# One block of expert 0 moved between the scores and y's products, in the sixth to tenth round of the attention stage

## The chip, the cores and the metric

The kernel runs on one core of one Trainium2 chip. The metric is the device time of one execution in microseconds (us); several executions are timed and their median is given. A profile of one further execution lists every instruction with its start and its duration. The engines are named as in the profile: PE is the matrix engine, PEld its weight loads, DVE the vector engine, ACT the scalar engine, POOL the general engine, SP the engine that issues most transfers.

## The reference

A linear attention with a decaying state gives `x`, and a mixture of eight experts with a balanced gate is applied to `x`.

```python
for t in range(S):                       # B, H, S, D = 4, 8, 768, 48
    cur = np.einsum('bhd,bhe->bhde', u[None] * kt, vt)
    y[:, :, t] = np.einsum('bhd,bhde->bhe', rt, state + cur)
    state = w[None, :, :, None] * state + np.einsum('bhd,bhe->bhde', kt, vt)
...
logits = x @ w_gate                      # x: 3072 x 384, 8 experts, F = 1024
P = np.exp(logits - logits.max())
for _ in range(8):
    P /= P.sum(1, keepdims=True) + 1e-09
    P /= P.sum(0, keepdims=True) + 1e-09
    P *= N / E
...
for e in range(E):
    h = np.maximum(x @ w1[e], 0.0)
    out += P[:, e:e + 1] * (h @ w2[e])
```

## The kernel before

The program has two stages. The first computes the attention; the second computes experts 1 to 7, with the products of PE back to back. Expert 0 is worked on during the first stage already, in small blocks that are strewn between the attention's steps. Every engine works through its own instructions strictly in the order in which the program wrote them (all calls go through a wrapper that keeps the program's order), and engines wait for each other at semaphores.

**Rounds.** The attention runs over 24 tiles of 128 tokens (6 per batch entry) in a loop over `i`. "Round 5" below is the round with `i == 5`, the sixth. Round `i` works on several tiles at once. On PE its order is: the transposes of tile `i+1` (`prT`, `pkT`, in `stage_b`), the scores of tile `i` (`pA`, in `stage_c`), the products of `y` for tile `i-1` (`py` from the state `S`, in `state_part`, where the tile isn't the first of its batch entry; then `py` from `vn` and the masked scores `at`, in `scores_part`), the state's new products of tile `i` (`py` from `vn` and `kp`, in `state_product`, where it isn't the last of its batch entry), and then blocks of expert 0.

**Expert 0's blocks.** A block is one entry of the list `units`, and `work(n)` issues the next n of them. A first-product block (`g1_unit`) is nine matmuls of 128x384 into a bank `ph`; a second-product block (`g2_half`) is twelve of them into a bank `po`. The bank `ph` comes from a pool with two buffers, so each `ph` block writes the bank of the last but one before it. A `ph` bank is read twice: ACT writes the high half `hb` from it, then DVE writes the low half (`hb<-ph,hb`). With `hold=True` these two reads are not issued at once but kept; in the next round `leave(0)` issues the ACT ones ahead of the copies `rT`, `kT`, and `leave(1)` the DVE ones after the row `dg` and ahead of the masked copy `at`. If a `po` block needs an `hb` that is still kept, `settle` issues what is kept on the spot.

**DVE in a round.** DVE's order is: `xsc` (low half of tile `i-2`), `dg`, the kept `hb` rows, the two masked copies `at<-mask,pA`, in some rounds a split of expert 0's weights (`ws`), then `x<-py,rk` (two rows), the state `S`, the maximum `xm`, three short rows that end with `xs`, and `kp` of a later tile. `x` is y's sum for tile `i-1` and needs the round's `py`. In some rounds `ws` comes behind `xs`.

**Which block is where.** Round 4 issues one block at its end, rounds 5 to 9 issue two, round 10 issues three; from round 11 on one stands between scores and y's products and two at the end. Blocks are numbered by group and chunk: `ph_0_3` is chunk 3 of group 0. Rounds 5 to 9 take `ph_0_1` and `ph_0_2`; `ph_0_3` and `po_0_0`; `po_1_0` and `po_2_0`; `ph_1_0` and `ph_1_1`; `ph_1_2` and `ph_1_3`.

Of the kernel before, what the change touches and what calls it, by code (L numbers as in the profile page):

```python
# [33 lines left out]
def rwkv_sinkhorn_moe(  # L34
# [37 lines left out]
    NE = 4  # L72
# [204 lines left out]
    def leave(n):  # L277
        for f in exits[n]:
            f()
        exits[n].clear()  # L280
        if n:
            owed.clear()
# [6 lines left out]
    def whole(gen):  # L289
        for _ in gen:  # L290
            pass
# [33 lines left out]
    def load_part(tt, nm, src):  # L325
        b, c = divmod(tt, NCHB)
        if tt == 3 and nm != "v":
            t_ = part(hb3, F32, 2880 + "rk".index(nm) * H * D, (H, D))
        else:
            t_ = ld.tile([P, H, D], F32, tag=nm + "n", name=f"{nm}n_{tt}", bufs=5 if nm == "v" else 3)  # L330
        Q.dma_start(t_, src[b, :, c * C : (c + 1) * C, :].rearrange("h t d -> t h d"))
        loads.setdefault(tt, {})[nm] = t_
# [197 lines left out]
    def prep(tt):  # L530
        ld_ = loads[tt]
        st[tt] = {}
        G.tensor_tensor(rp_[tt % 2][:, :, :D], ld_["r"], rt4, op=ALU.mult)
        if 0 < tt - 2 < NE:
            bonus(tt - 2)
        (G if 2 <= tt <= 2 * NE else V).tensor_tensor(kp_[tt % 3][:, :, :D], ld_["k"], kt4, op=ALU.mult)
        if tt == 2:
            bonus(0)

    def bonus_dot(tt):  # L540
        ld_ = loads[tt]
        rk = rk0
        if tt:
            rk = at2.tile([P, H, D], F32, tag="rk", name=f"rk_{tt}", bufs=3)
            G.tensor_tensor(rk, ld_["r"], ld_["k"], op=ALU.mult)
        G.tensor_tensor(rk, rk, ub, op=ALU.mult)
        st[tt]["rk"] = rk

    def bonus(tt):
        vn = loads[tt]["v"]  # L550
        dg = at2.tile([P, H], F32, tag="dg", name=f"dg_{tt}")
        V.tensor_reduce(dg, st[tt]["rk"], axis=AX.X, op=ALU.add)
        av = st[tt].pop("rk")
        G.tensor_tensor(av, vn, dg.unsqueeze(2).broadcast_to([P, H, D]), op=ALU.mult)
        if tt >= NE:
            aq = av.rearrange("p h d -> p (h d)")
            G.tensor_tensor(aq, aq, xadd(tt), op=ALU.add)
        st[tt]["av"] = av

    def stage_b(tt):  # L560
        d = st[tt]
        for nm, src in (("rT", rp_[tt % 2]), ("kT", kp_[tt % 3])):
            pool, tag = (ps2, "po") if tt <= NE + 1 else (ps3, "pa")
            pt = pool.tile([P, NPAIR, P], F32, tag=tag, name=f"p{nm}_{tt}")
            sv = src.rearrange("p (a j) d -> p a (j d)", j=2)
            for p_ in range(NPAIR):
                T.transpose(pt[:, p_, :], sv[:, p_, :], ident)
            dst = at2.tile([P, NPAIR, P], F32, tag=nm, name=f"{nm}_{tt}", bufs=3 if nm == "rT" else 2)
            S_.copy(dst, pt)
            d[nm] = dst  # L570

    def stage_c(tt):
        d = st[tt]
        rT, kT = d["rT"], d["kT"]
        at = at_[tt % 2].rearrange("p (a g) c -> p g a c", g=2)
        pas = []
        for g in range(2):
            pa = ps3.tile([P, NPAIR, C], F32, tag="pa", name=f"pA_{tt}_{g}")
            pas.append(pa)
        for a in range(NPAIR):  # L580
            for g in range(2):
                rows = slice(g * HP, g * HP + HP)
                for hs in (slice(0, HP), slice(HP, C)):
                    T.matmul(pas[g][hs, a, :], kT[rows, a, hs], rT[rows, a, :], start=True, stop=True)
        for g in range(2):
            V.copy_predicated(
                at[:, g], maski.unsqueeze(1).broadcast_to([P, NPAIR, C]), pas[g]
            )
# [38 lines left out]
    def addends(tt):  # L627
        d = st[tt]
        d["py"] = y_banks(tt)
        for n, x_ in enumerate((xadd(tt).rearrange("p (h d) -> p h d", d=D), d["av"])):  # L630
            xg = x_.rearrange("p (a g) d -> p g a d", g=2)
            for g in range(2):
                T.matmul(d["py"][g], ident, xg[:, g], start=(n == 0), stop=False, skip_group_check=True)
        if tt + 1 < NE:
            T.matmul(d["pu"], ident, st[tt + 1]["S"], start=False, stop=False, skip_group_check=True)

    def state_part(tt):
        d = st[tt]
        if tt % NCHB == 0:
            return  # L640
        fresh = "py" not in d
        if fresh:
            d["py"] = y_banks(tt)
        for p_ in range(NPAIR):
            for g in range(2):
                rows = slice(g * HP, (g + 1) * HP)
                for hs in (slice(0, HP), slice(HP, C)):
                    T.matmul(
                        d["py"][g][hs, p_, :], d["rT"][rows, p_, hs], d["S"][rows, p_, :],
                        start=(fresh and p_ == 0), stop=False, skip_group_check=True,  # L650
                    )
# [176 lines left out]
    def work(n, hold=False):  # L828
        held[0] = hold
        for _ in range(n):  # L830
            if units:
                whole(units.pop(0))
        held[0] = False
# [7 lines left out]
    def n_steps(i):  # L841
        return (0, 0) if i < 10 else (2, 2) if i < 21 else (3, 2)
# [6 lines left out]
    def run(i, place):  # L849
        for f in hooks.pop((i, place), []):  # L850
            f()
# [45 lines left out]
    def send_x(i):  # L897
        if 2 <= i <= NTT + 1 and i != TH + 1:
            scale_x(i - 2)
            if i > TH:  # L900
                stage_e(i - 2)
            emitted[0] = i - 1

    for i in range(NTT + 3):
        if 1 <= i <= NE:
            stage_b(i + 1)
        run(i, "turned")
        if i + 2 < NTT and i != TH + 1:
            prep(i + 2)
        if i > NE:  # L910
            send_x(i)
        leave(0)
        if i + 1 < NTT:
            bonus_dot(i + 1)
        if NE < i < NTT - 1:
            stage_b(i + 1)
        if 1 <= i <= NE:
            addends(i - 1)
        if i <= NE:
            send_x(i)  # L920
        n = i + 5 if i < 2 else i + 4
        if i != 2 and n < NTT:
            load_part(n, "r", r)
            load_part(n, "k", k)
        if i == 0:
            load_part(3, "v", v)
        if i == 8:
            Q.dma_start(wg, w_gate.rearrange("(c p) e -> p c e", p=P))
        run(i, "loads")
        if NE <= i < NTT:  # L930
            bonus(i)
        leave(1)
        run(i, "early")
        if i < NTT:
            stage_c(i)
        if i > 10:
            work(1)
        run(i, "masked")
        if 1 <= i <= NTT:
            state_part(i - 1)  # L940
            scores_part(i - 1)
        if 2 <= i <= TH + 1:
            turn_x(i - 2)
        if i < NTT:
            state_product(i)
        if 1 <= i <= NTT:
            sum_x(i - 1)
        if i < NTT:
            state_sum(i)
        if 1 <= i <= NTT:  # L950
            bound_x(i - 1)
        if i > NTT:
            work(2)
        run(i, "middle")
        if 2 <= i < NTT - 2:
            load_part(i + 2, "v", v)
        for _ in range(n_steps(i)[0]):
            prepare()
        if i <= NTT:
            if i > TH:  # L960
                work(1 if i == 4 else 3 if i == 10 else 2, hold=i < 10)
            elif i == 0:
                S_.copy(onesb, ones)
                S_.copy(ident16, ident)
        run(i, "end")
        for _ in range(n_steps(i)[1]):
            prepare()
        if i == TH:
            prep(i + 3)
            scale_x(TH - 1)  # L970
            run(i, "last")
            units += [g1_unit(0, fc, 0) for fc in range(FHC)]
            units += [g2_half(0, t, 0, 0) for t in range(TH)]
        done = i - 2
        if TH <= done < NTT and done % TH == TH - 1:
            po_ = done // TH
            for p_, j in ((1, 0), (0, 1), (1, 1)) if po_ == 1 else ((po_, 0), (po_, 1)):
                turn[0] += 1
                g1 = [g1_unit(p_, fc, turn[0]) for fc in range(j * FHC, (j + 1) * FHC)]
                units += merged(g1, [g2_half(*a_) for a_ in pend])  # L980
                pend = [(p_, t, j, turn[0]) for t in range(TH)]
# [402 lines left out]
    for s in range(NS):  # L1384
        tasks = stage_tasks(s)
        for g in range(NG):
            for j in range(2):
                for n, nxt in enumerate(g1_slots(s, g, j)):
# [3 lines left out]
                    i = j * NPR + n  # L1392
# [37 lines left out]
```

## Time and profile before

| | |
|---|---|
| median of 3 runs | 1513.77 us (1513.34 to 1514.48) |
| the profiled execution: its time | 1514.62 us |
| the profiled execution: its span | 1513.1 us |
| DVE busy over the span | 1010.1 us (67%) |
| ACT busy over the span | 674.8 us (45%) |
| POOL busy over the span | 586.8 us (39%) |

The profiled execution's own time is 1.5 us longer than its span, and 0.85 us above the median. Rows of a timeline begin with start and duration in us, then engine, operation, tile written and tiles read, shapes, and count of merged instructions; in brackets stands the idle time ahead of them and who ended it. "issue" is idle time for which the profile names no one. A row's duration of merged matmuls includes the drain of the last one, so the step from one row's start to the next row's start is what a part costs on PE.

### The profile page before, as it was taken

How to read it: one execution, taken by the hardware profiler on the slowest of the kernel's cores; microseconds unless marked ns; L12 is line 12 of the kernel's file. 1: busy time of each engine (PE TensorE's matmuls, PEld its weight loads, DVE VectorE, ACT ScalarE, POOL GpSimd, SP SyncE). 2: the span in 40 equal slices, each digit the busy share in tenths (PEclk: the TensorE clock that was granted, in tenths of full speed). 3: DMA queues.
4: the chain of work that ended last, by engine and by line, in shares of the span. 5: the costliest groups of instructions: out<-in, count | busy, mean ns of one | idle time of the engine just before them, and what ended most of it. 6: DMA issues, size and time to landing. Idle time of an engine off the chain costs nothing.

```text
span 1513.1 us, 28843 instructions
## 1 busy us (share of the span) xinstructions
PE 1501.1 (99%) x11654; PEld 846.7 (56%) x11656; DVE 1010.1 (67%) x1678; ACT 674.8 (45%) x1206; POOL 586.8 (39%) x687
## 2 busy tenths in 40 slices
PE   9999999999999999999999999999999999999999
PEld 7767766555555555555555555555555555555555
DVE  7998859676666666666676666666565666566464
ACT  6534425345354544445454544445353544444320
POOL 8878966200224243342425243242424233242200
PEclk9999999999999999999999999999999999999999
DMA  8965532212255576657666666655554454555434
GB/s 164 163 115 119 113 89 78 79 46 75 81 106 62 83 130 93 123 80 128 90 88 114 91 127 92 116 61 99 61 94 56 60 99 59 97 61 96 58 95 130
DMA packets 184840, 142.69 MB, mean 94 GB/s; under 512 B 107137, under 2 KB 178562, under 8 KB 184706
## 3 DMA queue, kind: packets, MB, share of 16 engines
q0 software_dynamic: 44928, 61.36, 32.6%
q1 hardware_dynamic: 139568, 79.48, 20.3%
q8 instruction: 91, 1.49, 0.4%
q14 instruction: 43, 0.35, 0.1%
q10 hardware_dynamic: 210, 0.00, 0.0%
HBM read 55.39 MB, written 80.23 MB: 90 GB/s over the span
## 4 chain that ended last, share of the span: by engine, by line
PE 95%; DVE 3%; POOL 1%; ACT 1%; issue 1%; ACTq 0%; POOLq 0%; DVEq 0%
PE po L30 49%; PE bZ L30 12%; PE bY L30 12%; PE ph L30 5%; PE bA L30 5%; PE bB L30 5%; PE py L30 2%; PE bC L30 2%; PE pA L30 1%; PE prT L30 1%; PE pkT L30 1%; POOL rk L30 0%; DVE hb L30 0%; DVE wms L30 0%; ACT hbx L30 0%
## 5 line engine op out<-in xcount | busy, mean ns | idle before, releaser
L30 PE MATMUL po<-ws,hbx 128*128 128x384 f16 x3360 | 736.8, 326 | 0.0
L30 POOL DMA_DIRECT2D accd<-stg x288 | 250.5, 870 | 694.8 <-ACT stg L30 673.9
L30 PEld LDWEIGHTS <-hbx 128*128 128x128 f16 x3360 | 328.8, 98 | 291.1
L30 PEld LDWEIGHTS <-ws 128*128 128x128 f16 x3096 | 301.0, 98 | 247.4 <-issue 3.5
L30 ACT ACTIVATE hbx<-tb 128x512 f16<-128x512 f32 x224 | 141.0, 630 | 450.8 <-DVE tb L30 450.8
L30 PE MATMUL po<-ws,hb 128*128 128x384 f16 x1248 | 323.2, 326 | 0.5 <-DVE hb L30 0.5
L30 DVE TENSOR_TENSOR tb<-bY,tb 128x512 f32<-128x512 f32 x168 | 116.2, 692 | 176.6 <-PE bY L30 175.0
L30 ACT ACTIVATE stg<-po,pe 128x384 f32<-128x384 f32 x312 | 179.1, 574 | 122.7 <-PE po L30 95.0
L30 PE MATMUL bZ<-xv,ws 128*128 128x512 f16 x840 | 227.0, 379 | 0.7 <-DVE tb L30 0.7
L30 PE MATMUL bY<-xv,ws 128*128 128x512 f16 x840 | 227.0, 379 | 0.0
L30 DVE TENSOR_TENSOR tb<-bZ,tb 128x512 f32<-128x512 f32 x168 | 115.5, 687 | 135.4 <-PE bZ L30 135.4
L30 PEld LDWEIGHTS <-hb 128*128 128x128 f16 x1248 | 121.1, 98 | 95.2 <-DVE hb L30 1.3
L30 POOL TENSOR_TENSOR ucb<-rawb 128x256 f32<-128x256 f32 x84 | 77.5, 972 | 112.7 <-DMA rawb<-in_moe_w_dram 112.7
L30 DVE TENSOR_TENSOR tb<-bB,tb 128x512 f32<-128x512 f32 x112 | 77.5, 692 | 49.2 <-PE bB L30 47.3
L30 PE MATMUL ph<-hbx,ws 128*128 128x384 f16 x576 | 104.2, 326 | 0.6 <-issue 0.3
L30 DVE SCALAR_TENSOR_TENSOR hb<-tb,hbx 128x512 f16<-128x512 f32 x112 | 77.3, 690 | 24.6 <-ACT hbx L30 19.5
L30 PE MATMUL bB<-xv,ws 128*128 128x512 f16 x336 | 90.8, 379 | 0.0
L30 PE MATMUL bA<-xv,ws 128*128 128x512 f16 x336 | 90.8, 379 | 0.0
L30 DVE SCALAR_TENSOR_TENSOR hbx<-tb,hbx 128x512 f16<-128x512 f32 x112 | 78.1, 698 | 14.7 <-ACT hbx L30 10.4
L30 ACT COPY tb<-bZ 128x512 f32<-128x512 f32 x56 | 32.8, 586 | 65.5 <-PE bZ L30 65.4
L30 ACT ACTIVATE hb<-ph 128x384 f16<-128x384 f32 x64 | 31.0, 489 | 58.6 <-PE ph L30 58.2
L30 DVE SCALAR_TENSOR_TENSOR hb<-ph,hb 128x384 f16<-128x384 f32 x64 | 34.8, 550 | 29.2 <-ACT hb L30 28.7
(181 smaller groups left out, 1492.9 us busy)
## 6 DMA issues: line engine op xcount, KB each, us to landing
accd<-stg POOLq DMA_DIRECT2D x288, 192.0 KB, 3.7
rawb<-in_moe_w_dram SPq DMA_DIRECT2D x28, 768.0 KB, 7.9
e0d<-stg SPq DMA_DIRECT2D x48, 192.0 KB, 1.9
hb<-e0d SPq DMA_DIRECT2D x48, 192.0 KB, 3.7
vn<-in_v_dram SPq DMA_DIRECT2D x24, 192.0 KB, 4.4
accd<-stg SPq DMA_DIRECT2D x24, 192.0 KB, 1.8
accd<-hb POOLq DMA_DIRECT2D x24, 192.0 KB, 4.7
rawb<-accd SPq DMA_DIRECT2D x24, 192.0 KB, 2.4
```

What stands on the lines that cost most here:

```text
L30: return lambda *a, **k: self.tc.keep_in_program_order(f(*a, **k))
```

## The change

In rounds 5 to 9 the first of the two blocks is issued ahead of y's products, still with its reads kept for later; only one is left at the round's end. Rounds 0 to 4 and from 10 on are as they were.

```diff
@@ -933,8 +933,8 @@
         run(i, "early")
         if i < NTT:
             stage_c(i)
-        if i > 10:
-            work(1)
+        if i > NE and i != 10:
+            work(1, hold=i < 10)
         run(i, "masked")
         if 1 <= i <= NTT:
             state_part(i - 1)
@@ -958,7 +958,7 @@
             prepare()
         if i <= NTT:
             if i > TH:
-                work(1 if i == 4 else 3 if i == 10 else 2, hold=i < 10)
+                work(1 if i < 10 else 3 if i == 10 else 2, hold=i < 10)
             elif i == 0:
                 S_.copy(onesb, ones)
                 S_.copy(ident16, ident)
```

Round 6 on PE, before: `pA` are the scores of tile 6, `py_5` the products of y for tile 5, `ph_0_3` and `po_0_0` the round's blocks.

```order
L30 MATMUL pA_6_1_1149<-rT_6_988,kT_6_995 64x128 x2
L30 MATMUL py_5_0_1168<-S1_179,rT_5_819 64x48 [waits Activation_49]
...
L30 MATMUL py_5_0_1168<-vn_6_961,kp0_173 32x48 x15
L30 LDWEIGHTS ws1_75
L30 MATMUL ph_0_3_1246<-hbx_72,ws1_75 128x384 [waits DVE_49]
...
L30 MATMUL po_0_0_1258<-ws1_75,hb3_73 128x384
```

The same place on PE in the changed program:

```order
L30 MATMUL pA_6_1_1149<-rT_6_988,kT_6_995 64x128 x2
L30 LDWEIGHTS ws1_75
L30 MATMUL ph_0_3_1168<-hbx_72,ws1_75 128x384 [waits DVE_49]
...
L30 MATMUL py_5_0_1178<-S1_179,rT_5_819 64x48 [waits Activation_49]
...
L30 MATMUL py_5_0_1178<-vn_6_961,kp0_173 32x48 x15
...
L30 MATMUL po_0_0_1258<-ws1_75,hb3_73 128x384
```

The nine matmuls of `ph_0_3`, which wait for DVE, have moved from behind y's products to ahead of them; `po_0_0` has stayed.

Round 9 on PE in the changed program, with y's products of tile 8 and the blocks `ph_1_2` and `ph_1_3`:

```order
L30 MATMUL pA_9_1_1618<-rT_9_1435,kT_9_1442 64x128 x2
L30 LDWEIGHTS ws1_75
L30 MATMUL ph_1_2_1637<-hbx_72,ws1_75 128x384 [waits DVE_49]
...
L30 MATMUL py_8_0_1648<-S1_179,rT_8_1288 64x48 [waits Activation_49]
...
L30 MATMUL py_8_0_1648<-vn_9_1400,kp0_173 32x48 x15
L30 LDWEIGHTS ws1_75
L30 MATMUL ph_1_3_1727<-hbx_72,ws1_75 128x384 [waits DVE_49]
```

Here too the first block now stands, with its wait for DVE, ahead of y's products.

Round 9 on DVE in the changed program, from the low half of tile 7 to the sum of tile 8:

```order
L30 SCALAR_TENSOR_TENSOR xsc_7_1582<-x_7_1553,xs_7_1560,xsc_7_1582 128x384 [waits DMAHW1_49,Activation_49]
L30 TENSOR_REDUCE dg_9_1609<-rk_9_1427 128x8 [waits Pool_49]
L30 SCALAR_TENSOR_TENSOR hb3_73<-ph_1_0_1477,hb3_73 128x384 [waits Activation_49]
L30 SCALAR_TENSOR_TENSOR hb3_73<-ph_1_1_1570,hb3_73 128x384 [waits Activation_49]
L30 COPY_PREDICATED at1_177<-mask_168,pA_9_0_1617 128x4x128 [waits PE_49]
L30 COPY_PREDICATED at1_177<-mask_168,pA_9_1_1618 128x4x128 [waits PE_49]
L30 SCALAR_TENSOR_TENSOR ws1_75<-ws0_74,sw0_1_114,ws1_75 128x768 [waits DMAHW6_49,Activation_49]
L30 TENSOR_TENSOR x_8_1714<-py_8_0_1648,rk_8_1280 128x4x48 [waits PE_49,Pool_49]
```

On DVE, ACT, POOL and SP no instruction has moved in any round: only the numbers in names differ from before. The reads of `ph_1_0` and `ph_1_1` stand where they stood.

## The prediction

> **What bounds the kernel now.** First I read the page's head, then a table of stretches around the changed rounds, then the timelines of PE and DVE in them. Rounds are numbered by `i`: round 5 is the sixth.
>
> ```profile
> span 1513.1 us, 28843 instructions
> PE 1501.1 (99%) x11654; PEld 846.7 (56%) x11656; DVE 1010.1 (67%) x1678; ACT 674.8 (45%) x1206; POOL 586.8 (39%) x687
> ...
> 40.00:88.00 48.00, 45.39 (x1084) 33.29 (x1084) 44.97 (x97) 21.45 (x37) 37.84 (x39) 1.00 0.87 157
> 88.00:1513.00 1425.00, 1418.99 (x9758) 785.55 (x9755) 934.65 (x1521) 626.35 (x1115) 514.20 (x603) 1.00 0.52 90
> ...
> 45.00:53.00 8.00, 6.71 (x186) 5.03 (x185) 7.90 (x12) 3.89 (x6) 7.84 (x7) 1.00 1.19 207
> ```
>
> The columns of the stretches are length, then PE, PEld, DVE, ACT and POOL busy. After 88 us PE is busy 1418.99 of 1425 us, so whatever start round 11 gets (87.85 us before) moves the end by as much. Between 40 and 88 us, which holds the five changed rounds and round 10, DVE is as full (44.97 of 48) as PE (45.39). DVE's share of 67% over the span says nothing there: this is the stretch in which both lie on the path by turns.
>
> PE in rounds 5 to 7:
>
> ```profile
> 41.22 1.10 PE L30 MATMUL pA<-rT,kT 64*64 64x128 f32 x32
> ...
> 49.16 0.63 PE L30 MATMUL py<-S,rT 64*64 64x48 f32 x32
> ...
> 51.46 0.33 PE L30 MATMUL py<-vn,at 128*32 128x48 f32 x11 [0.96 <-issue]
> ...
> 52.10 1.64 PE L30 MATMUL ph<-hbx,ws 128*128 128x384 f16 x9
> 53.58 2.25 PE L30 MATMUL po<-ws,hb 128*128 128x384 f16 x12
> 55.66 0.60 PE L30 MATMUL prT<-ident,rp 128*128 128x128 f32 x4
> ```
>
> DVE in the same stretch:
>
> ```profile
> 44.17 0.62 DVE L30 TENSOR_TENSOR x<-py,rk 128x192 f32<-128x192 f32 x2
> ...
> 45.87 3.35 DVE L30 SCALAR_TENSOR_TENSOR ws<-ws,sw,ws 128x768 f16<-128x768 f32 x2
> 49.14 1.37 DVE L30 SCALAR_TENSOR_TENSOR xsc<-x,xs,xsc 128x384 f16<-128x384 f32 x1
> ...
> 50.90 1.01 DVE L30 SCALAR_TENSOR_TENSOR hb<-ph,hb 128x384 f16<-128x384 f32 x2
> ...
> 53.06 0.62 DVE L30 TENSOR_TENSOR x<-py,rk 128x192 f32<-128x192 f32 x2
> ...
> 54.90 0.54 DVE L30 SCALAR_TENSOR_TENSOR hb<-ph,hb 128x384 f16<-128x384 f32 x1
> 55.35 1.30 DVE L30 TENSOR_TENSOR kp<-kn,ktab 128x384 f32<-128x384 f32 x1
> ```
>
> The reader is to see two things. DVE has no bracket in any of these rows: it runs from x of round 5 to the end without a pause. And PE's `ph` of round 6 (52.10) starts 0.7 us after the first `hb<-ph,hb` of the pair is done (50.90 and half of 1.01, 51.40). That DVE row frees the bank which `ph_0_3` writes. Before, the block came late enough not to notice.
>
> PE in rounds 8 to 10, then DVE:
>
> ```profile
> 62.74 0.60 PE L30 MATMUL prT<-ident,rp 128*128 128x128 f32 x4
> ...
> 64.35 1.10 PE L30 MATMUL pA<-rT,kT 64*64 64x128 f32 x32
> ...
> 67.22 0.38 PE L30 MATMUL py<-vn,kp 128*32 128x48 f32 x17 [0.33 <-issue]
> ...
> 70.46 0.60 PE L30 MATMUL prT<-ident,rp 128*128 128x128 f32 x4
> ...
> 73.62 0.53 PE L30 MATMUL py<-vn,kp 128*32 128x48 f32 x32
> 74.08 3.10 PE L30 MATMUL ph<-hbx,ws 128*128 128x384 f16 x18
> 77.01 0.60 PE L30 MATMUL prT<-ident,rp 128*128 128x128 f32 x4
> ...
> 84.26 0.34 PE L30 MATMUL ph<-hbx,ws 128*128 128x384 f16 x1 [0.23 <-DVE ws L30]
> ```
>
> ```profile
> 67.73 0.62 DVE L30 TENSOR_TENSOR x<-py,rk 128x192 f32<-128x192 f32 x2 [0.86 <-PE py L30]
> ...
> 71.55 1.36 DVE L30 SCALAR_TENSOR_TENSOR xsc<-x,xs,xsc 128x384 f16<-128x384 f32 x1
> ...
> 73.29 1.01 DVE L30 SCALAR_TENSOR_TENSOR hb<-ph,hb 128x384 f16<-128x384 f32 x2
> ...
> 76.37 0.62 DVE L30 TENSOR_TENSOR x<-py,rk 128x192 f32<-128x192 f32 x2
> ...
> 79.28 1.35 DVE L30 SCALAR_TENSOR_TENSOR xsc<-x,xs,xsc 128x384 f16<-128x384 f32 x1
> ...
> 83.21 0.99 DVE L30 SCALAR_TENSOR_TENSOR ws<-ws,sw,ws 128x768 f16<-128x768 f32 x1
> ```
>
> In round 8 DVE waits for PE (0.86 us, until the last `kp` product at 67.22 + 0.38 = 67.60 is done: a hand-over of 0.13 us). From 67.73 to 84.20 it doesn't stop, and PE's last `ph` matmul at 84.26 waits for it (hand-over 0.06). So the old path is: PE to x of round 8, DVE to `ws` of round 10, PE from there on. Round 9's `ph` pair (74.08) again starts just after its bank is freed (73.29 and half of 1.01, 73.79).
>
> **The change, part by part.** No work is added. PE's order alone changes, and a block in the middle is already there in round 12, whose rows give the prices:
>
> ```profile
> 97.72 1.10 PE L30 MATMUL pA<-rT,kT 64*64 64x128 f32 x32
> 98.76 1.64 PE L30 MATMUL ph<-hbx,ws 128*128 128x384 f16 x9
> 100.33 0.68 PE L30 MATMUL py<-S,rT 64*64 64x48 f32 x32
> 100.94 0.89 PE L30 MATMUL py<-vn,at 128*32 128x48 f32 x64
> 101.64 0.50 PE L30 MATMUL py<-vn,kp 128*32 128x48 f32 x26
> ```
>
> From start to start: scores 1.04, block 1.57, `py` from `S` 0.61, from `vn` 0.70; the `kp` products take 0.53 (73.62). At the round's end a block takes 1.47 (half of 77.01 - 74.08). What the block delays is `py`, and behind it DVE's x; what it gains is cover for waits. I follow the path, which alternates between legs of DVE, taken as long as before, and legs of PE.
>
> - *Round 5.* `ph_0_1` finds its bank free (the maximum that read it ended in round 4). x starts at 41.22 + 1.04 + 1.57 + 0.61 + 0.89 + 0.13 = 45.46 instead of 44.17. **+1.29.** DVE had no pause behind x, so all of it reaches the `hb` pair: the first is done at 52.69 instead of 51.40.
> - *Round 6.* PE is through the scores at about 49.2 (old `py` start) and meets `ph_0_3`, whose bank is freed only at 52.69: **a new wait of about 3.4 us**, with `py`, the `kp` products, `po_0_0` and the whole next round queued behind it, and DVE's x behind `py`. The 0.96 us of "issue" idle at 51.46 falls inside that wait, so its cover is worth nothing. From `hb` done to x: 0.06 + 1.57 + 0.61 + 0.70 + 0.53 + 0.13 = 3.60, before 53.06 - 51.40 = 1.66. **+1.94.** Then DVE's row at 54.90 frees `po_0_0`'s last matmul and round 7 (55.66 follows 55.35 by 0.31): same as before, shifted by 3.23.
> - *Round 7.* Two `po` blocks, banks free; one block stands between scores and `py`, 1.57 - 1.47 = **+0.10**. PE sets the pace here.
> - *Round 8.* From its first transposes to x: 64.35 - 62.74 = 1.61, then 1.04 + 1.57 + 0.61 + 0.70 + 0.53 + 0.13, in all 6.19; before 67.73 - 62.74 = 4.99 with the 0.33 us of idle in it. **+1.20**, if that idle is covered by the block; 0.3 to 0.5 more if it comes again.
> - *Round 9.* x of round 8 is 4.53 late, so `hb` is done at 78.32. PE is through its scores at about 75.5 and waits for the bank of `ph_1_2`: **a second wait of about 2.8 us**. From `hb` to x 3.60 again, before 76.37 - 73.79 = 2.58. **+1.02.**
> - *Round 10.* DVE from x to `ws` as before (7.83), PE's `ph` behind it. **0**; PE's waits for ACT ahead of `py` there are off the path before and after.
>
> Sum 1.29 + 1.94 + 0.10 + 1.20 + 1.02 = 5.55, call it **+5.5 us**, at the start of round 11, and from there PE carries it to the end. Bounds: each PE leg is a sum of rows that vary by 0.1, five legs 0.5; the idle of round 8 adds up to 0.5, an idle that falls away later could take 0.7 off. DVE's legs are the larger unknown (next part). ACT is busy 21.45 of 48 us and its copies `rT`, `kT` are done long before the delayed `py`, so ACT costs nothing here; SP and POOL keep their order, and are hidden by DVE as before.
>
> The profiled execution would go from 1514.62 (span 1513.1) to about 1520.1; the median, 0.85 lower, from 1513.77 to **1519.3**. Some 0.2% (3 us) is about what a measurement of this kernel can tell from no change.
>
> [...] The first row that bears on DVE's legs: two `ws` take 3.35 us at 45.87, where POOL is busy 7.84 of 8 us, while one takes 0.99 at 83.21. [...]
>
> **The rivals.**
>
> *DVE's legs shorten.* The rows slide by 1.3 to 4.5 us against POOL. If the two `ws` of round 5 came to stand free, 3.35 - 1.98 = 1.37 is saved: +4.2, 1518.0. Against it: POOL is full in that stretch and waits for nothing that is moved.
>
> *Not slower.* If beside that all three `xsc` on the path (1.37, 1.36, 1.35) fell to what one takes where it stands free, the legs lose 1.37 + 2.28 = 3.65:
>
> ```profile
> 29.90 0.60 DVE L30 SCALAR_TENSOR_TENSOR xsc<-x,xs,xsc 128x384 f16<-128x384 f32 x1
> ```
>
> Then +1.9, 1515.7, no change that can be told; with the 0.7 us of a later idle gone too, 1515.0. It decides itself at about 2.5 us saved on DVE's legs: from there the change isn't slower by 0.2%. For it speaks that DVE now pauses and POOL may get ahead of it; against it, that POOL's rows behind `dg` wait for DVE and slide along with it. For a real gain the bank waits would have to be absent, and even then x is late by 1.29 in round 5 and 1.20 in round 8, with DVE full between.
>
> *The delay grows.* If the "issue" idles come again behind the new waits (0.96 in round 6, 0.33 in round 8, both on PE's legs then): +6.9, 1520.7.
>
> **How the numbers follow.** Forecast 0.60 (1517.8 to 1520.6); shorter legs 0.15 (1518.0); not slower 0.15 (about 1515.7, of it 0.03 for a real gain); longer 0.10 (1520.7 and above). The range 1515.6 to 1521.2 leaves out about half of the third and some of the last, nearly 2 in 10. Faster by over 0.2%: 0.03; within 0.2%: 0.13; slower: 0.84.
>
> **What would show it.** In the changed profile PE should wait in front of a `ph` row, ended by DVE `hb`, for some 3.4 us near 49 us and 2.8 us near 75 us; the "issue" idle in the `vn` row of round 6 should be gone. DVE should pause ahead of its x rows in all five rounds (1.3 us in round 5, about 1.9 in round 6). Round 11's first transposes should come at 93.4 instead of 87.85, and all later landmarks as much later. I am wrong if the `ph` rows in the middle start right behind `pA` in rounds 6 and 9, or if PE's time after 88 us shrinks.

## The result, and the profile after

The changed kernel takes 1523.21 us (median of 6 executions, 1521.29 to 1525.37), the kernel before 1514.12 us in the same session (1513.34 to 1514.75): +9.1 us, a ratio of 1.0060 (95% interval 1.0049 to 1.0071). The forecast was 1519.3 with a range up to 1521.2. The direction and both new waits came as forecast; the loss is larger than the range allowed.

The profiled execution took 1522.87 us. The head of its page, and the chain of work that ended last, by engine:

```profile
span 1521.4 us, 28846 instructions
PE 1504.1 (99%) x11656; PEld 847.9 (56%) x11656; DVE 1008.4 (66%) x1678; ACT 674.3 (44%) x1206; POOL 586.3 (39%) x687
...
PE 94%; DVE 3%; POOL 1%; issue 1%; ACT 1%; ACTq 0%; DVEq 0%; POOLq 0%
```

PE is busy 3.0 us longer (1504.1 against 1501.1) although it has the same instructions (the weight loads are as many, 11656; the trace of before lacks two matmul records). That is the first sign that something besides a wait has been added. The timeline of PE, rounds 5 to 7:

```profile
41.61 1.10 PE L30 MATMUL pA<-rT,kT 64*64 64x128 f32 x32
...
52.44 2.00 PE L30 MATMUL ph<-hbx,ws 128*128 128x384 f16 x9 [3.25 <-DVE hb L30]
54.37 1.11 PE L30 MATMUL py<-S,rT 64*64 64x48 f32 x32
55.41 1.51 PE L30 MATMUL py<-vn,at 128*32 128x48 f32 x64
56.69 0.64 PE L30 MATMUL py<-vn,kp 128*32 128x48 f32 x32
57.27 1.96 PE L30 MATMUL po<-ws,hb 128*128 128x384 f16 x11
59.92 0.34 PE L30 MATMUL po<-ws,hb 128*128 128x384 f16 x1 [0.69 <-DVE hb L30]
60.09 0.60 PE L30 MATMUL prT<-ident,rp 128*128 128x128 f32 x4
```

And from round 8's start to round 11's:

```profile
67.27 0.60 PE L30 MATMUL prT<-ident,rp 128*128 128x128 f32 x4
...
80.01 2.25 PE L30 MATMUL ph<-hbx,ws 128*128 128x384 f16 x9 [2.81 <-DVE hb L30]
82.19 1.11 PE L30 MATMUL py<-S,rT 64*64 64x48 f32 x32
83.23 1.35 PE L30 MATMUL py<-vn,at 128*32 128x48 f32 x64
84.40 0.52 PE L30 MATMUL py<-vn,kp 128*32 128x48 f32 x32
...
96.75 0.60 PE L30 MATMUL prT<-ident,rp 128*128 128x128 f32 x4
```

The two waits are there, 3.25 and 2.81 us (forecast 3.4 and 2.8), both ended by DVE's `hb`. But look at the steps from row to row behind them: in round 6 the block takes 1.93, `py` from `S` 1.04, from `vn` 1.28, where round 12 of before had 1.57, 0.61 and 0.70; in round 9 it is 2.18, 1.04 and 1.17. The same instructions are slower there, and only there. The table of stretches (length, PE busy, then the granted clock of PE, 1.00 being full) says why:

```profile
52.40:54.40 2.00, 1.96 (x13) 0.79 0.82 123
54.40:57.30 2.90, 2.90 (x130) 0.56 1.10 191
57.30:60.00 2.70, 2.01 (x16) 1.00 0.04 8
...
80.00:82.20 2.20, 2.19 (x11) 0.69 0.64 122
82.20:85.00 2.80, 2.80 (x130) 0.63 1.03 190
85.00:87.00 2.00, 2.00 (x16) 1.00 0.03 6
```

After each pause the clock that PE is granted falls, to 0.65 and 0.66 on average over the five microseconds, and comes back to 1.00. DVE's rows give the landmarks between:

```profile
45.77 0.62 DVE L30 TENSOR_TENSOR x<-py,rk 128x192 f32<-128x192 f32 x2 [0.68 <-PE py L30]
...
47.48 2.71 DVE L30 SCALAR_TENSOR_TENSOR ws<-ws,sw,ws 128x768 f16<-128x768 f32 x2
...
51.85 1.01 DVE L30 SCALAR_TENSOR_TENSOR hb<-ph,hb 128x384 f16<-128x384 f32 x2
...
57.48 0.62 DVE L30 TENSOR_TENSOR x<-py,rk 128x192 f32<-128x192 f32 x2 [3.37 <-PE py L30]
...
73.86 0.62 DVE L30 TENSOR_TENSOR x<-py,rk 128x192 f32<-128x192 f32 x2 [2.10 <-PE py L30]
...
79.41 1.01 DVE L30 SCALAR_TENSOR_TENSOR hb<-ph,hb 128x384 f16<-128x384 f32 x2
...
85.06 0.83 DVE L30 TENSOR_TENSOR x<-py,rk 128x192 f32<-128x192 f32 x2 [2.48 <-PE py L30]
...
92.09 1.02 DVE L30 SCALAR_TENSOR_TENSOR ws<-ws,sw,ws 128x768 f16<-128x768 f32 x1
```

Start times against those of before, and what each leg of the path added:

| landmark | before | after | late by | leg added | forecast |
|---|---|---|---|---|---|
| round 5, scores (PE) | 41.22 | 41.61 | 0.39 | 0.39 | 0 |
| round 5, x (DVE) | 44.17 | 45.77 | 1.60 | 1.21 | 1.29 |
| round 6, `hb` pair (DVE) | 50.90 | 51.85 | 0.95 | -0.65 | 0 |
| round 6, x (DVE) | 53.06 | 57.48 | 4.42 | **3.47** | 1.94 |
| round 7, transposes (PE) | 55.66 | 60.09 | 4.43 | 0.01 | 0 |
| round 8, transposes (PE) | 62.74 | 67.27 | 4.53 | 0.10 | 0.10 |
| round 8, x (DVE) | 67.73 | 73.86 | 6.13 | 1.60 | 1.20 |
| round 9, `hb` pair (DVE) | 73.29 | 79.41 | 6.12 | -0.01 | 0 |
| round 9, x (DVE) | 76.37 | 85.06 | 8.69 | **2.57** | 1.02 |
| round 10, `ws` (DVE) | 83.21 | 92.09 | 8.88 | 0.19 | 0 |
| round 11, transposes (PE) | 87.85 | 96.75 | 8.90 | 0.02 | 0 |
| end of the span | 1513.1 | 1521.4 | 8.3 | -0.6 | 0 |

The two legs behind the waits added 1.53 and 1.55 us more than forecast, 3.1 together. Everything else stays within 0.7 of its term, and together it comes to -0.3. The -0.6 at the end is idle time without a named cause, 1.1 us before and 0.4 after. The other signs that the prediction named came as well: DVE pauses ahead of x in all five rounds (0.68, 3.37, 1.95, 2.10 and 2.48 us), and the 0.96 us of idle in round 6 is gone.

### The profile page after: what moved, and what is told of

Read it like the earlier page. It is cut to its first block, busy times and chain, and to the rows that moved or that the text cites. A ratio compares the mean times of both kernels' runs of the same rounds, so it can differ in the third digit from the quotient of the medians.

```text
span 1521.4 us, 28846 instructions
## 1 busy us (share of the span) xinstructions
PE 1504.1 (99%) x11656; PEld 847.9 (56%) x11656; DVE 1008.4 (66%) x1678; ACT 674.3 (44%) x1206; POOL 586.3 (39%) x687
## 4 chain that ended last, share of the span: by engine, by line
PE 94%; DVE 3%; POOL 1%; issue 1%; ACT 1%; ACTq 0%; DVEq 0%; POOLq 0%
PE po L30 48%; PE bZ L30 12%; PE bY L30 12%; PE ph L30 5%; PE bA L30 5%; PE bB L30 5%; PE py L30 2%; PE bC L30 2%; PE pA L30 1%; PE prT L30 1%; PE pkT L30 0%; DVE hb L30 0%; POOL rk L30 0%; DVE wms L30 0%; ACT hbx L30 0%
## 5 line engine op out<-in xcount | busy, mean ns | idle before, releaser
L30 DVE TENSOR_TENSOR tb<-bB,tb 128x512 f32<-128x512 f32 x112 | 77.4, 691 | 49.2 <-PE bB L30 47.3
```

The source lines that it names most:

```text
L30: return lambda *a, **k: self.tc.keep_in_program_order(f(*a, **k))
```

## The experiments

Theory A: the bank wait costs twice, once as the delay that was forecast and once because PE's clock falls behind the pause. Theory B: the slow rows have another cause. Theory C: a block ahead of y's products costs by itself, bank or not. The kernel before ran beside each set: 1514.59 us for the first four, 1514.06 for the next four, 1514.28 for the last two.

### The pause filled

```diff
+        if i in (6, 9):
+            spin(10)
         if i > NE and i != 10:
             work(1, hold=i < 10)
```

> The changed kernel, with ten idle-work matmuls of 128x512 (about 0.21 us each, their output is never read) ahead of the middle block of rounds 6 and 9, where PE stands still for 3.25 and 2.81 us in the changed kernel's profile. Theory A (the bank wait costs twice: once as delay, once because PE's granted clock halves for some 3 us after it): PE's pauses shrink to about 1 us, the granted clock stays at 1.000 over the span, the py rows behind the two blocks take 0.61, 0.70 and 0.46 us again from start to start, and the time falls by about 3 us against the changed kernel, to about 1519.5 to 1520.5 (+5.5 to +6.5 against before). Theory B (those rows are slow for another reason, such as the fetch of instructions or the transfers beside them): they stay slow, and the time stays at about 1523.

Measured: 1519.27 us (1518.66 to 1520.09), ratio 1.0033 (1.0020 to 1.0045), granted clock 1.000 in all six executions. PE's timeline of round 6:

```profile
49.51 2.33 PE L30 MATMUL pz<-zeros 128*128 128x512 f16 x10
53.05 1.62 PE L30 MATMUL ph<-hbx,ws 128*128 128x384 f16 x9 [1.20 <-DVE hb L30]
54.60 0.68 PE L30 MATMUL py<-S,rT 64*64 64x48 f32 x32
55.21 0.89 PE L30 MATMUL py<-vn,at 128*32 128x48 f32 x64
55.91 0.52 PE L30 MATMUL py<-vn,kp 128*32 128x48 f32 x32
```

The block still waits for the same DVE row, but it now takes 1.55, and the rows behind it 0.61 and 0.70. Twenty useless matmuls make the changed kernel 3.9 us faster (4.4 when each is set against the kernel beside it). What is left, +4.7 against the kernel beside it, is the forecast's +5.5 less 0.8. DVE's rows of the filled kernel show the two legs behind the waits by themselves:

```profile
47.53 3.26 DVE L30 SCALAR_TENSOR_TENSOR ws<-ws,sw,ws 128x768 f16<-128x768 f32 x2
...
52.45 1.01 DVE L30 SCALAR_TENSOR_TENSOR hb<-ph,hb 128x384 f16<-128x384 f32 x2
...
56.58 0.62 DVE L30 TENSOR_TENSOR x<-py,rk 128x192 f32<-128x192 f32 x2 [1.85 <-PE py L30]
...
78.50 1.01 DVE L30 SCALAR_TENSOR_TENSOR hb<-ph,hb 128x384 f16<-128x384 f32 x2
...
82.63 0.83 DVE L30 TENSOR_TENSOR x<-py,rk 128x192 f32<-128x192 f32 x2 [0.96 <-PE py L30]
```

Against the starts of before, `hb` of round 6 is 1.55 late and x 3.52; in round 9 it is 5.21 and 6.26. The legs add 1.97 and 1.05, where 1.94 and 1.02 were forecast: at full clock the forecast's prices hold to 0.03 us. Theory B is out.

### The middle block where the bank is free, and where it isn't

Rounds 5, 7 and 8 alone (in the second run: 6 and 9 alone); the other rounds issue both blocks at their end.

```diff
-        if i > NE and i != 10:
+        if i in (5, 7, 8) or i > 10:
             work(1, hold=i < 10)
...
-                work(1 if i < 10 else 3 if i == 10 else 2, hold=i < 10)
+                work(1 if i in (4, 5, 7, 8) else 3 if i == 10 else 2, hold=i < 10)
```

> The middle block only in rounds 5, 7 and 8, where its bank is free; rounds 6 and 9 as before the change. Theory A: no wait of a ph row for hb, clock 1.000; x is late by 1.2 in round 5, 0.1 in round 7 and 1.2 to 1.6 in round 8, DVE carries it: +2.3 to +3.0 against before, 1516.5 to 1517. Theory C (what costs is that a block stands ahead of y's products at all, bank or not): three of five rounds carry three fifths of the loss, +5 or more, 1519 or above.

> The middle block only in rounds 6 and 9, where its bank is still taken; rounds 5, 7 and 8 as before the change. Theory A: two waits of ph for hb, but shorter, about 2.2 us each, since DVE is not late from round 5 and 8; x late by 1.9 and 1.0. If a wait of 2.2 us leaves the clock alone: +3.0, 1517; if the clock falls after it as after 2.8 and 3.3 us: another 1.5 for each, +6, 1520. Theory C: two fifths of the loss, +3.6.

Measured: rounds 5, 7 and 8 cost +2.1 (1516.69 us; ratio 1.0012, 1.0003 to 1.0022), clock 1.000 in every execution, no wait of a `ph` row for `hb`. Rounds 6 and 9 cost +2.6 (1517.17; 1.0018, 1.0009 to 1.0027). Together that is 4.7, what the filled kernel shows, though the second still holds some falls of the clock. In the profile of rounds 6 and 9 alone PE's pauses are shorter:

```profile
51.57 3.04 PE L30 MATMUL ph<-hbx,ws 128*128 128x384 f16 x9 [2.41 <-DVE hb L30]
54.53 0.85 PE L30 MATMUL py<-S,rT 64*64 64x48 f32 x32
55.32 0.89 PE L30 MATMUL py<-vn,at 128*32 128x48 f32 x64
...
77.00 1.62 PE L30 MATMUL ph<-hbx,ws 128*128 128x384 f16 x9 [1.35 <-DVE hb L30]
```

After 2.41 us of pause the block took 2.96 (54.53 - 51.57) instead of 1.57, and the rows behind it were back at 0.79 and 0.70; after 1.35 us nothing happened. Over the eleven executions the mean clock was 0.999 in five and 1.000 in six, so this pause doesn't always bring the clock down; the five are 0.7 us slower in the median than the six. Theory A's number without a fall (+3.0) is nearer than with two (+6). Theory C's +3.6 for this kernel lies inside the interval (+1.4 to +4.1), so this run doesn't settle it; its +5 for the other is refuted.

### The low reads a row earlier

```diff
         leave(0)
+        if i in (6, 9):
+            leave(1)
```

> The changed kernel, with DVE's kept low reads (hb) of rounds 6 and 9 issued ahead of xsc and dg instead of behind them, so the banks come free about 1.7 us earlier. Theory A: waits of about 1.7 us in round 6 and 1 us or none in round 9, no fall of the clock, x late by what the block itself costs: +3 against before, 1517. Theory C: the order of DVE's rows changes nothing in what stands ahead of y: still about 1523.

Measured: 1520.35 us (1520.02 to 1521.77; ratio 1.0042, 1.0028 to 1.0056), 3 us slower than I expected. The expectation was wrong about the edit: in these rounds `send_x` stands ahead of `leave(0)`, so the reads passed `dg` (0.46 us) but not `xsc`. The pauses were 2.46 and 2.35 us, and in the profile the clock fell behind the second and not behind the first. As a test of the bank it says little; as one more pair of pauses it is of use below.

### A free bank for the two blocks

```diff
-        ph = ps1.tile([P, TB], F32, tag="ph", name=f"ph_{po_}_{fc}")[:, :TB0]
+        pool, tag = (ps2, "po") if (po_, fc) in ((0, 3), (1, 2)) else (ps1, "ph")
+        ph = pool.tile([P, TB], F32, tag=tag, name=f"ph_{po_}_{fc}")[:, :TB0]
```

First with the change as it is, then with the middle block in rounds 6 and 9 only.

> The changed kernel, but the two blocks that met a taken bank (ph_0_3 in round 6, ph_1_2 in round 9) write a bank of the other pool (tag po), which is free in those rounds. Nothing else moves. Theory A (the bank wait and the clock behind it): no ph row waits for hb, clock 1.000; x stays late by about 1 in round 5, 0.1 in round 7 and 1.2 to 1.6 in round 8, rounds 6 and 9 are set by DVE and add nothing: +2 to +3 against before, about 1517. Theory C (a block ahead of y's products costs by itself, in every round): all five rounds still pay, +5 or more, 1519.5 or above.

> As the kernel before with the middle block in rounds 6 and 9 only, and these two blocks on a free bank. Theory A: no wait for hb, x not late, since DVE is behind PE there: 0 to +0.5 against before; the 0.96 us of idle in round 6 is covered but buys nothing, as DVE sets the start of round 7. Theory C: +3 or more. If the covered idle did count, it would be faster than before by up to 1.

Measured, rounds 6 and 9 only: 1514.28 us, ratio 1.0000 (0.9991 to 1.0009). The same two moves that cost 2.6 us on a taken bank cost nothing on a free one. PE's rows of round 6:

```profile
48.82 1.64 PE L30 MATMUL ph<-hbx,ws 128*128 128x384 f16 x9
...
55.32 0.34 PE L30 MATMUL po<-ws,hb 128*128 128x384 f16 x1 [1.19 <-DVE hb L30]
55.49 0.60 PE L30 MATMUL prT<-ident,rp 128*128 128x128 f32 x4
```

The block starts right behind the scores and the old 0.96 us of idle time is gone, but PE gives it back, 1.19 us, in front of the last matmul that needs DVE's `hb`: round 7 starts where it did. This is the bound by DVE that the prediction read from DVE's rows without a pause.

Measured, the whole change on free banks: 1517.61 us (1515.84 to 1519.42), ratio 1.0021 (1.0011 to 1.0032): +3.5, above the 2 to 3 expected, with a mean clock of 0.998 to 1.000. Its profile shows where the excess is:

```profile
83.08 0.32 PE L30 MATMUL py<-S,rT 64*64 64x48 f32 x4 [1.74 <-ACT rT L30]
...
84.17 1.23 PE L30 MATMUL py<-vn,at 128*32 128x48 f32 x64
85.16 0.88 PE L30 MATMUL py<-vn,kp 128*32 128x48 f32 x32
85.97 2.59 PE L30 MATMUL ph<-hbx,ws 128*128 128x384 f16 x9
```

PE, freed of its waits, runs ahead to round 10, stands there for 1.74 us until ACT's copy `rT` is done (it stands in ACT's queue behind `xsc`, which starts at 81.18, just after DVE's `xs` ends at 81.10), and is slow behind that pause: `py` from `vn` 0.99, the block 2.43. From `ws` of round 10 to the start of round 11 it takes 5.80 us instead of 4.64. The fall of the clock isn't shown to be all of the excess: of the two executions at a mean clock of 1.000 one took 1515.84 us and the other 1517.62.

### A round that PE paces, and a smaller dose

Round 7 alone with the middle block (`if i == 7 or i > 10`), and the changed kernel with `spin(4)` in place of `spin(10)`.

> The middle block in round 7 only, where both banks are free and PE sets the pace (a second-product block). Theory A: +0.1 for one more change between large and small matmuls, x late by 2.0 to 2.5 in that round but made up by DVE's pauses in round 8: 0 to +0.5 against before. Theory C: a fifth of the loss, +1.8.

> The changed kernel with four idle-work matmuls (about 0.9 us) ahead of the blocks of rounds 6 and 9, so that PE's pauses are about 2.4 and 1.9 us. A dose between the changed kernel (3.25 and 2.81 us; 0.996 to 0.999 of the clock) and ten matmuls (1.2 and 0.5 us; 1.000). [...]

Measured: round 7 alone 1514.41 us, ratio 1.0004 (0.9995 to 1.0012): no change that can be told. Theory C's +1.8 lies at the upper end of this interval; what refutes it is the run with rounds 6 and 9 on free banks (0 instead of +3). With four filling matmuls 1520.91 us (1520.50 to 1526.25), ratio 1.0051 (1.0037 to 1.0064): three executions at 1.000 of the clock, the others at 0.999, 0.998 and 0.998. Pauses of 1.87 and 1.83 us left the clock alone in the profiled execution; by the mean clocks it fell somewhere in three others, of which there is no trace.

### DVE relieved

If DVE paces rounds 8 to 10, work taken off it must show at the end. Four products `kp` go to POOL (in the second run together with the middle block in rounds 6 and 9 on a free bank):

```diff
-        (G if 2 <= tt <= 2 * NE else V).tensor_tensor(kp_[tt % 3][:, :, :D], ld_["k"], kt4, op=ALU.mult)
+        (G if 2 <= tt <= 3 * NE else V).tensor_tensor(kp_[tt % 3][:, :, :D], ld_["k"], kt4, op=ALU.mult)
```

> The kernel before, with four products kp (tiles 9 to 12, rounds 7 to 10, 0.55 to 1.30 us each on DVE) computed on POOL instead of DVE; PE's order as before. If DVE's row of work from x of round 8 to the weights' split of round 10 sets the start of round 11, as theory A says, that row gets 1 to 2 us shorter and PE's waits in round 10 (0.54, 0.17, 0.23 us) go: -0.5 to -1.5 against before, 1512.6 to 1513.6. If POOL's own row gets in the way (full until 66.6 us): 0 or slower. Theory C says nothing on it.

> The same with the middle block in rounds 6 and 9 on a free bank. Theory A: with DVE relieved, the covered idle of round 6 may count: equal to the other or up to 1 us faster, 1512 to 1513.5. Theory C: 3 us or more slower than the other.

Measured: 1512.12 us, ratio 0.9985 (0.9976 to 0.9994), 2.2 us faster than before and the fastest kernel of this study; with the two moved blocks 1513.23, ratio 0.9998 (0.9989 to 1.0007): 1.1 us slower than without them, where 0 to 1 us faster was expected. DVE's rows of the first:

```profile
71.38 1.00 DVE L30 SCALAR_TENSOR_TENSOR hb<-ph,hb 128x384 f16<-128x384 f32 x2
...
74.51 0.63 DVE L30 TENSOR_TENSOR x<-py,rk 128x192 f32<-128x192 f32 x2
...
81.00 1.00 DVE L30 SCALAR_TENSOR_TENSOR ws<-ws,sw,ws 128x768 f16<-128x768 f32 x1
```

`ws` of round 10 starts at 81.00 instead of 83.21, 2.2 us earlier, and the time falls by as much. Of the 2.2 us, 1.6 come between x of round 8 (67.11 instead of 67.73) and `ws`, the other 0.6 ahead of x. The four rows that left DVE are those of rounds 6 to 9 in the trace, not of 7 to 10. With the two moved blocks DVE waits for PE ahead of x of round 9:

```profile
75.61 0.62 DVE L30 TENSOR_TENSOR x<-py,rk 128x192 f32<-128x192 f32 x2 [0.85 <-PE py L30]
```

That is 1.10 us later than without them (74.51): once DVE has time to spare, the delay of x that a middle block brings counts again.

## Why the prediction was right in its path and wrong in its size

- *What bounds the kernel* (DVE from x of round 8 to `ws` of round 10, PE after it): right. Relieving DVE by four rows moved `ws` by 2.2 us and the time by 2.2, 1.6 of it on that leg.
- *Round 5, +1.29*: 1.21. The `ws` pair behind it took 2.71 instead of 3.35, which gave back 0.65: the first rival in part, but not where POOL left a gap, for POOL was busy beside the pair for all of its 2.71 us, as before for 3.32 of the 3.40 us from 45.8 to 49.2. In the filled kernel the pair took 3.26 at nearly the same place (47.53), so this is no steady gain, and its cause wasn't tried. That a row of DVE gets shorter where POOL leaves it free was my estimate from a few rows and no run tests it: the `xsc` of 0.60 us at 29.90 has POOL busy for 0.44 us of it, and in the changed kernel the three `xsc` of the second rival took 1.35, 1.34 and 1.35 us.
- *Rounds 7 and 8, +0.10 and +1.20*: 0.10 and 1.60; the 0.4 in round 8 lies ahead of its scores, where PE now waits 0.24 us for an ACT copy. Rounds 5, 7 and 8 alone cost 2.1, measured by themselves.
- *The two bank waits*: there, at 3.25 and 2.81 us, and their cause is shown: on a free bank rounds 6 and 9 cost nothing.
- *The size of rounds 6 and 9, +1.94 and +1.02*: this is the step that failed. I priced PE's leg behind the wait with the rows of round 12, and bounded it with "rows that vary by 0.1". Those rows come from a PE that hadn't paused, and what a pause does to the rows behind it was put at nothing. Measured were 3.47 and 2.57, and the surplus of 3.1 us is the lowered clock: it agrees with PE's busy time (3.0 us more) and with the mean clock (0.998 of a span of 1521.4 us, 3.0 us, or 2.3 to 3.8 by the rounding). With the pauses filled the clock stayed full and the legs added 1.97 and 1.05.
- *The forecast time, 1519.3*: that the filled kernel took 1519.27 us is in part luck. It is +4.7 against the kernel beside it, not +5.5; and in its profile round 11 starts 6.47 us late, while everything behind that start is 1.6 us shorter than in the profile of before. In the rival of a growing delay the sum 5.55 + 0.96 + 0.33 gives 6.84, not 6.9, which changes nothing.

The spread fits too. In the six executions of the changed kernel the mean clock went from 0.999 (1521.29 us) to 0.996 (1525.37 us): three thousandths of the span are 4.6 us, and the times differ by 4.1. Taken back to 1.000, the six give 1519.0 to 1519.8, beside the filled kernel's 1519.27. That is an estimate: the means also hold a fall that costs no time, in the last 3.8 us, where PE has nothing left to do (in the profile of before the clock is 0.59 on average from 1512.0 us to the end at 1513.1, after PE's last matmul at 1509.01: 0.45 us of the span; in that of the changed kernel it is 0.98 over the last 3.8 us, 0.08 us). And a mean of 0.996 is some 6 us lost, more than two falls of 1.5 us; what happened in that execution no trace shows.

No rival in the prediction named the clock: the forecast pause of 3.4 us was priced as a wait and no more. In the changed kernel's profile the granted clock is 0.50 from 53.6 to 56.8 us and from 80.9 to 84.2 us. The length of a pause doesn't decide by itself whether the clock falls: in the profiled executions it fell after 3.25, 2.81, 2.41, 2.35 and 1.74 us (the last with a further wait of 0.17 us close behind), and not after 2.46, 1.87, 1.83, 1.47 us or any shorter one between 40 and 100 us. What else decides was not shown.

What stays open: why a pause of 2.41 us brings the clock down in some executions and not in others, and the 0.39 us by which round 5 began later in the changed kernel's profile. It lies ahead of everything that the change moves, and the other kernels' profiles show starts of the same scatter (round 5's transposes at 40.06 to 41.20 us).

## What to carry to other kernels

Before a block of matmuls is moved forward, look up which row of another engine frees the bank that it writes, and where that row stands in its queue: a block on a taken bank blocks all that is queued behind it (PE stood for 3.25 and 2.81 us here), and the same two blocks on a free bank cost nothing, where on the taken one they cost 2.6 us (a block in the middle of rounds 5, 7 and 8 still cost 2.1 us, as it delays what the next engine waits for). A pause of PE is to be priced with what may come behind it: here the clock fell behind five pauses of 1.74 to 3.25 us and stayed full behind three of 1.83 to 2.46 us, and each fall cost about 1.5 us in the profiles. Filling the pause with useless matmuls is a cheap way to see that part alone (3.9 us here). And idle time of PE that is covered buys nothing where the next engine in line has no pause: here taking four rows off DVE gave 2.2 us, covering PE's idle gave none.

## What the runs showed of the hardware that was not expected

The granted clock of PE fell not only behind pauses of 3.25 and 2.81 us but also behind 2.41, 2.35 and 1.74 us, by the mean clocks in some executions of a kernel and not in others (with rounds 6 and 9 alone 0.999 in five and 1.000 in six). The fall can come late: in the changed kernel most of the block's nine matmuls in round 6 still ran at full speed (the clock is 1.00 up to 53.5 us, the block starts at 52.44), while with rounds 6 and 9 alone the block was slow from its start (2.96 us). Each fall in the profiles stretched PE's rows by about 1.5 us; in the changed kernel the clock stood at 0.50 for 3.2 and 3.3 us. And a kernel whose waits are removed can pause elsewhere and pay there, as the 1.74 us in round 10 of the change on free banks show.
